# Attention backward as one stream of slots, and a guard moved from the MLP-down stage into the MLP forward

## The chip, the cores and the metric

The kernel runs on one core of one Trainium2 chip. The metric is the device time of one execution in microseconds (us). Medians are of several executions; one execution of each kernel comes with a profile and a trace. On one core the engines are TensorE (PE in the profile, with PEld for its weight loads, which overlap), VectorE (DVE), ScalarE (ACT), GpSimd (POOL) and SyncE (SP, which here only issues DMAs). Tiles lie in SBUF, the core's memory for them; matmuls write into PSUM buffers, which ACT and DVE read.

## The reference, cut to what matters

The program is a forward pass and its gradients: a layer norm, an attention block with 32 heads, a gated MLP whose output gates the attention's output, and the gradients of everything.

```python
x  = A_x                                   # [1, 2048, 576]
xn = layernorm(x)
# attention, H = 32 heads, Dh = 128, 2048 queries and keys; k_cache and v_cache are inputs
q  = (xn @ wq) -> heads
p  = softmax(q @ k_cache^T * Dh**-0.5)
s  = (p @ v_cache -> rows) @ wo
# MLP, F = 4608
h  = sigmoid(xn @ w_gate) * (xn @ w_up)
g  = silu(h @ w_down)
out = x + s * g
# returned: out and the gradients for x, k_cache, v_cache, wq, wo, w_gate, w_up, w_down
```

Of the kernel before, what the change touches and what calls it, by code (L numbers as in the profile page):

```python
# [95 lines left out]
def kernel(  # L96
# [72 lines left out]
    with tc.tile_pool(name="pa", bufs=1) as pa:  # L169
        wd_sb = pa.tile([P, FT, D], bf, name="wd_sb")  # L170
        with tc.tile_pool(name="a1w", bufs=1) as wp:
# [22 lines left out]
            with tc.tile_pool(name="a0", bufs=3) as sb0, tc.tile_pool(name="a0ps", bufs=2, space=PSUM) as ps0, \  # L194
# [23 lines left out]
                for grp in range(NFC // GRP):  # L218
                    for st in range(NT):
# [9 lines left out]
                        for c in range(GRP):  # L229
# [13 lines left out]
                            nc.scalar.activation(oma[:], g_ps[:], AF.Sigmoid, scale=-1.0)  # L243
                            nc.vector.tensor_tensor(h_row[:, cs], u_ps[:], a_row[:, cs], op=ALU.mult)
# [5 lines left out]
            a0x.release()  # L250

# [3 lines left out]
        with tc.tile_pool(name="gd", bufs=2) as gp:  # L255
            ksq = gp.tile([P, H], f32, name="ksq", bufs=1)
            wsq = gp.tile([P, DT], f32, name="wsq", bufs=1)
            nc.vector.memset(wsq[:], 0.0)

            def guard_k(h):  # L260
                kt_ = gp.tile([P, NT * P], bf, name="gk")
                nc.gpsimd.dma_start(kt_[:], A_k_cache[0, h].rearrange("(p t) d -> p (t d)", t=NT))
                nc.scalar.activation(kt_[:], kt_[:], AF.Square, accum_out=ksq[:, h:h + 1])

            def guard_w(i):
                d0, kd = dts[i]
                wt_ = gp.tile([P, HD], bf, name="gw")
                nc.gpsimd.dma_start(wt_[:kd, :], A_wq[d0:d0 + kd, :])
                nc.scalar.activation(wt_[:kd, :], wt_[:kd, :], AF.Square, accum_out=wsq[:kd, i:i + 1])

            def guard_end():
                gm = gp.tile([P, 2], f32, name="gm", bufs=1)
                nc.vector.tensor_reduce(gm[:, 0:1], ksq[:], axis=AX.X, op=ALU.max)
                nc.vector.tensor_reduce(gm[:, 1:2], wsq[:], axis=AX.X, op=ALU.add)
                nc.sync.dma_start(gd_d[0:1, :].rearrange("o p -> p o"), gm[:, 0:1])
                nc.sync.dma_start(gd_d[1:2, :].rearrange("o p -> p o"), gm[:, 1:2])
                gr = gp.tile([1, 2, P], f32, name="gr", bufs=1)
                nc.sync.dma_start(gr[:], gd_d[:, :].rearrange("(o a) p -> o a p", o=1))
                gs = gp.tile([1, 4], f32, name="gs", bufs=1)
                nc.vector.tensor_reduce(gs[:, 0:1], gr[:, 0, :], axis=AX.X, op=ALU.max)  # L280
                nc.vector.tensor_reduce(gs[:, 1:2], gr[:, 1, :], axis=AX.X, op=ALU.add)
                nc.vector.tensor_tensor(gs[:, 2:3], gs[:, 0:1], gs[:, 1:2], op=ALU.mult)
                nc.vector.tensor_scalar(gs[:, 3:4], gs[:, 2:3], (SAFE / SCALE) ** 2 / D, None, op0=ALU.is_le)
                nc.vector.tensor_copy(flag_i[:], gs[:, 3:4])

            with tc.tile_pool(name="a2h", bufs=4) as hp, \
                    tc.tile_pool(name="a2s", bufs=2) as sb, tc.tile_pool(name="a2ps", bufs=2, space=PSUM) as ps, \
                    tc.tile_pool(name="a2pt", bufs=2, space=PSUM) as pst:
                SG = ldiv(NT, 2)
                pend2 = []  # L290
                for sg in range(NT // SG):
                    grows = slice(sg * SG * P, (sg + 1) * SG * P)
                    got = sb.tile([P, SG, D], bf, name="got")
                    nc.gpsimd.dma_start(got[:], go2[grows, :].rearrange("(t p) d -> p t d", p=P))
                    g2 = sb.tile([P, SG, D], f32, name="g2")
                    dsil = sb.tile([P, SG, D], bf, name="dsil")
                    g2b = sb.tile([P, SG, D], bf, name="g2b")
                    ds_t = sb.tile([P, SG, D], bf, name="ds_t")
                    for sl in range(SG):
                        st = sg * SG + sl  # L300
                        srows = slice(st * P, (st + 1) * P)
                        hT_st = hp.tile([P, FT, P], bf, name="hT_st")
                        nc.sync.dma_start_transpose(hT_st[:], h_d[srows, :])
                        while len(pend2) > 1:
                            (t_, sl_, st_) = pend2.pop(0)
                            transpose_to(nc, pst, t_[:, sl_, :], D, dsT, st_ * P, ident, alt)
                        for j in range(st * H // NT, (st + 1) * H // NT):
                            guard_k(j)
                        if st < DT:
                            guard_w(st)  # L310
                        accs = [ps.tile([P, 512], f32, name=f"acc{j}") for j in range(len(ncs))]
                        for ft in range(FT):
                            for j, (n0, nn) in enumerate(ncs):
                                nc.tensor.matmul(accs[j][:, :nn], lhsT=hT_st[:, ft, :], rhs=wd_sb[:, ft, n0:n0 + nn],
                                                 start=(ft == 0), stop=(ft == FT - 1))
                        sig = sb.tile([P, D], f32, name="sig")
                        for j, (n0, nn) in enumerate(ncs):
                            nc.scalar.activation(sig[:, n0:n0 + nn], accs[j][:, :nn], AF.Sigmoid)
                            nc.vector.tensor_tensor(g2[:, sl, n0:n0 + nn], accs[j][:, :nn], sig[:, n0:n0 + nn], op=ALU.mult)
                        t1 = sb.tile([P, D], f32, name="t1")  # L320
                        nc.vector.scalar_tensor_tensor(t1[:], sig[:], 1.0, g2[:, sl, :], op0=ALU.subtract, op1=ALU.mult)
                        nc.vector.tensor_tensor(dsil[:, sl, :], sig[:], t1[:], op=ALU.subtract)
                        nc.vector.tensor_tensor(ds_t[:, sl, :], got[:, sl, :], g2[:, sl, :], op=ALU.mult)
                        pend2.append((ds_t, sl, st))
                    nc.gpsimd.tensor_copy(g2b[:], g2[:])
                    nc.gpsimd.dma_start(g2_d[grows, :].rearrange("(t p) d -> p t d", p=P), g2b[:])
                    nc.gpsimd.dma_start(dsil_d[grows, :].rearrange("(t p) d -> p t d", p=P), dsil[:])
                    nc.gpsimd.dma_start(ds_d[grows, :].rearrange("(t p) d -> p t d", p=P), ds_t[:])

                for (t_, sl_, st_) in pend2:  # L330
                    transpose_to(nc, pst, t_[:, sl_, :], D, dsT, st_ * P, ident, alt)
                guard_end()
# [6 lines left out]
    def attention(fast):  # L339
        with ExitStack() as es:  # L340
# [11 lines left out]
            skew = SKEW if fast else 2  # L352
# [82 lines left out]
            def prep_dot(hs, sc):  # L435
                if sc == 0:
                    hs.dOT = ld1.tile([P, S], bf, name="dOT")
                    hs.dOn = ld1.tile([P, NT, P], bf, name="dOn")
                gen_T(hs.woT, dsT, hs.dOT, sc, "v")
                nb = CH // P  # L440
                pe_transpose_blocks(lambda j: hs.dOT[:, j * P:(j + 1) * P], sc * nb, (sc + 1) * nb,
                                    lambda g, n: hs.dOn[:, g:g + n, :], "v")
# [10 lines left out]
            def scores(hs, qt, hf):  # L453
                qs = slice(qt * P, (qt + 1) * P)
                with tc.high_priority():
                    sp = ps_big.tile([P, HW_], f32, name="sp", tag="big")
                    for c in range(HW_ // CH):
                        nc.tensor.matmul(sp[:, c * CH:(c + 1) * CH], lhsT=hs.QT[:, qs],  # L458
                                         rhs=hs.KT[:, hf * HW_ + c * CH: hf * HW_ + (c + 1) * CH], start=True, stop=True)
                return sp  # L460

            def main1(hs, qt):
                Pq = slabp.tile([P, S], bf, name="Pq")
                hs.slabs[qt] = Pq
                rsp = stat.tile([P, NHF], f32, name="rsp")
                if fast:
                    for hf in range(NHF):
                        sp = scores(hs, qt, hf)
                        nc.scalar.activation(Pq[:, hf * HW_:(hf + 1) * HW_], sp[:], AF.Exp, scale=SCALE,  # L469
                                             accum_out=rsp[:, hf:hf + 1])  # L470
                else:
                    nm = stat.tile([P, NHF], f32, name="nm")
                    snegs = []
                    for hf in range(NHF):
# [424 lines left out]
```

## The kernel before: what the change touches

The stages run one after the other: MLP forward, MLP-down (with its gradient `ds`), attention for 32 heads (forward and backward, 61% of the time), then four stages of output projection and weight gradients, which the change leaves alone. All code and diffs in this document are condensed; `...` marks a cut, and lines that only name or index things are left out without a mark.

A *guard* decides at run time whether softmax may skip its row maximum: it needs a bound on the largest squared norm of a key and the sum of squares of `wq`. It reads 21 MB, squares it on ACT and sums it. Before, all of that sat inside the MLP-down stage, whose own input `hT_st` is a DMA transpose of `h`:

```python
def guard_k(h):                                   # one head's keys, 512 KB
    kt_ = gp.tile([P, NT * P], bf, name="gk")     # gp has 2 buffers
    nc.gpsimd.dma_start(kt_[:], A_k_cache[0, h].rearrange("(p t) d -> p (t d)", t=NT))
    nc.scalar.activation(kt_[:], kt_[:], AF.Square, accum_out=ksq[:, h:h + 1])
...
    hT_st = hp.tile([P, FT, P], bf, name="hT_st")           # MLP-down, 16 row tiles
    nc.sync.dma_start_transpose(hT_st[:], h_d[srows, :])
    ...
    for j in range(st * H // NT, (st + 1) * H // NT):
        guard_k(j)                                          # two heads per row tile
    if st < DT:
        guard_w(st)
    for ft in range(FT): ...                                # 72 matmuls
```

Attention works head by head in two phases of 16 query tiles (`qt`) of 128 rows. Phase 1 makes the scores `sp` in two halves of 1024 keys, takes the exponential on ACT into a slab `Pq` (128x2048), and transposes the slab by DMA (`PT`) for the product with V. Phase 2 makes `dp` in two halves, multiplies it into the slab on ACT and DVE, and transposes the slab again (`dST`) for the product with K. Between these come many narrow matmuls of 128 columns: tails (`acc<-Vn,PT` and `acc<-Kn,dST`), and the sums for the gradients of V and K (`acc<-dOn,Pq`, `acc<-Qn,Pq`).

```python
skew = 5                         # a slab's tail comes 5 tiles after its scores
def scores(hs, qt, hf):
    with tc.high_priority():     # the scheduler may put these ahead of other matmuls
        sp = ps_big.tile([P, HW_], f32, name="sp", tag="big")      # 2 PSUM buffers, shared with dp
        for c in range(HW_ // CH):
            nc.tensor.matmul(sp[:, c*CH:(c+1)*CH], lhsT=hs.QT[:, qs], rhs=hs.KT[...], ...)
def main2(hs, qt):
    for hf in range(NHF):
        with tc.high_priority(): dp = ...                           # 2 matmuls, as above
        if hf == NHF - 1:
            nc.vector.scalar_tensor_tensor(Pq[:, hsl], dp[:], hs.delta[...], Pq[:, hsl], op0=ALU.subtract, op1=ALU.mult)
        else:
            nc.scalar.activation(t[:], dp[:], AF.Identity, bias=hs.negdelta[...], scale=1.0)
            nc.vector.tensor_tensor(Pq[:, hsl], t[:], Pq[:, hsl], op=ALU.mult)
    hs.dST[qt] = transpose_slab(hs, qt, "dST")                      # DMA transpose on SP
def post1(hs):                                                      # start of phase 2
    nc.gpsimd.tensor_scalar(hs.rsc[:], hs.rinv_all[:], SCALE, None, op0=ALU.mult)
    nc.gpsimd.tensor_tensor(hs.Qn[:], hs.Qn[:], hs.rsc[:].unsqueeze(2).to_broadcast([P, NT, P]), op=ALU.mult)
...
for h in range(H):                 # the loop
    for i in range(NT + skew):     # phase 1: main1(i), tail1(i - skew), parts of dK of the head before, dV
        ...
    for i in range(NT + skew):     # phase 2: main2(i), tail2(i - skew), rest of dV, dK, next head's preparation
        ...
```

## Time and profile before

The median is 5703.88 us (5701.29 to 5713.11, 3 runs; 5705.36 with a fourth). The profiled run spans 5680.1 us. The stages, from the starts of their last matmuls in the trace (worked out from the trace's records, as are all per-head figures below):

| stage | us before | ends at |
|---|---|---|
| MLP forward | 346.2 | 346.2 |
| MLP-down, with the guard | 251.5 | 597.7 |
| attention | 3487.9 | 4085.6 |
| the rest | 1594.5 | 5680.1 |

The table of stretches of the kernel before gives busy time per engine in each stretch, then the granted clock of TensorE, the busy share of the DMA engines and GB/s:

```profile
45.00:347.00 302.00, 300.02 (x1398) 137.64 (x1425) 163.27 (x321) 184.26 (x327) 74.64 (x138) 1.00 0.52 201
347.00:605.00 258.00, 167.15 (x1208) 84.45 (x1232) 62.20 (x106) 94.34 (x122) 60.66 (x85) 0.82 0.94 198
605.00:4090.00 3485.00, 3314.47 (x39843) 2521.31 (x40352) 1849.14 (x4223) 2049.67 (x3585) 1013.70 (x1759) 1.00 1.06 188
```

The columns are PE, PEld, DVE, ACT, POOL. The MLP forward is PE-bound (300 of 302 us). The MLP-down stage is not: PE works 167 of 258 us while the DMA engines are 94% busy. Its waits say on what (engine, line, what it waited for: us in total, times, longest):

```profile
ACT gk L263 <- DMA gk<-in_A_k_cache_dram: 74.3, 16, 11.8
PE acc L314 <- DMA hT_st<-h_d: 44.0, 5, 22.2
```

In attention PE looks 95% busy, yet records of matmuls overlap (a 128-column one lasts 219 ns on average where the next starts 56 ns later), so that hides what is lost. The timeline shows starts; `acct` are transposes of 128x128 blocks made on PE. The kernel before on PE, first in phase 1, then in phase 2 (start us, us, engine, line, operation, out<-in, how many in a row, idle before and its releaser):

```profile
2702.41 0.59 PE L458 MATMUL sp<-KT,QT 128*128 128x512 bf16 x2
2702.84 0.66 PE L369 MATMUL acct<-ident,QT 128*128 128x128 bf16 x9
2703.42 0.59 PE L458 MATMUL sp<-KT,QT 128*128 128x512 bf16 x2
2703.85 0.33 PE L369 MATMUL acct<-ident,QT 128*128 128x128 bf16 x3
2704.01 0.44 PE L562 MATMUL acc<-dOn,Pq 128*128 128x128 bf16 x5
2704.42 0.59 PE L458 MATMUL sp<-KT,QT 128*128 128x512 bf16 x2
...
2727.08 1.22 PE L500 MATMUL acc<-Vn,PT 128*128 128x128 bf16 x19
2728.49 1.02 PE L523 MATMUL dp<-VT,dOT 128*128 128x512 bf16 x4 [0.19 <-ACT t L529]
2729.35 1.22 PE L500 MATMUL acc<-Vn,PT 128*128 128x128 bf16 x19
2730.77 0.38 PE L523 MATMUL dp<-VT,dOT 128*128 128x512 bf16 x1 [0.19 <-ACT t L529]
```

A score half comes every 1.00 us: the scores run ahead in a burst as fast as ACT's exponentials (one per 1.00 us) free the two PSUM buffers. In phase 2 four `dp` matmuls come at once and then wait for ACT and DVE. The next lines are waits of the kernel before between 630 and 4060 us. The first shows the end of each burst: ACT has no free slab and waits up to 12.8 us, once a head, until the matmuls on old slabs have freed one.

```profile
ACT Pq L469 <- PE acc L562: 395.3, 31, 12.8
PEld L523 <- issue: 152.2, 514, 0.7
PE dp L523 <- ACT t L529: 57.9, 294, 0.5
PE acct L369 <- DVE dOT L42: 31.2, 64, 0.8
```

Matmuls that follow each other without a wait start every 55.8 ns with 128 columns and every 215.2 to 215.8 ns with 512, which is N/2.4 + 2.45 ns (N columns). Summed over the 40,352 matmuls of the attention that is 3111 us; from first to last start the trace has 3475 us. So 364 us are stalls of PE: by the trace about 190 us before `dp`, 135 us before `sp`, the rest mostly before the `dOT` transposes.

### The profile page before, as it was taken

To read this page: it belongs to the slowest core of one execution; us is meant where nothing else is said; L and a number is where in the kernel's file an instruction comes from. 1 tells how busy PE (TensorE), PEld (TensorE's weight loads), DVE (VectorE), ACT (ScalarE), POOL (GpSimd) and SP (SyncE) were. 2 spreads that over 40 slices of the span, in tenths; PEclk is the share of its full clock that TensorE was granted. 3 is DMA by queue.
4 is the path that set the end of the run, shared out by engine and by line. 5 is a ranking of instruction groups with operands and counts; after the bars stand their busy time and mean duration, and the time that the engine had idled before them with its cause. 6 is when DMAs were issued, how large, how long until landed. Compare 5 with 4: busy or idle time off the path is not lost.

```text
span 5680.1 us, 129804 instructions
## 1 busy us (share of the span) xinstructions
PE 5290.7 (93%) x54473; PEld 3695.7 (65%) x55220; DVE 2472.9 (44%) x5723; ACT 2601.1 (46%) x4668; POOL 1429.2 (25%) x2398
## 2 busy tenths in 40 slices
PE   8977899999999999999999999999789999999999
PEld 3433577777777777777777777777656777744454
DVE  5532445545545555554554554555433333211011
ACT  7543565565565555555556556556422222200000
POOL 2222223223223323322322322322212222211000
PEclk9988999999999999999999999999999999999999
DMA  7489899999999999999999999999955555583875
GB/s 275 182 214 207 159 188 186 191 191 184 190 187 188 190 188 188 188 190 187 185 194 187 187 191 190 184 189 186 213 174 169 174 174 174 178 240 123 179 148 111
DMA packets 2715209, 1053.93 MB, mean 186 GB/s; under 512 B 2521185, under 2 KB 2641634, under 8 KB 2711986
## 3 DMA queue, kind: packets, MB, share of 16 engines
q1 hardware_dynamic: 2626050, 743.33, 72.4%
q0 software_dynamic: 88560, 302.14, 16.9%
q8 instruction: 434, 7.11, 0.5%
q14 instruction: 165, 1.35, 0.1%
HBM read 213.91 MB, written 201.00 MB: 73 GB/s over the span
## 4 chain that ended last, share of the span: by engine, by line
PE 60%; ACT 18%; issue 12%; DVE 3%; DMA 3%; POOL 2%; SPq 1%; ACTq 0%; POOLq 0%; DVEq 0%
PE acc L562 11%; ACT Pq L469 9%; PE acc L840 7%; ACT t L529 7%; PE dp L523 5%; PE accw L768 5%; PE acc L500 5%; PE acc L537 5%; PE sp L458 4%; PE acc L427 3%; PE dh L745 3%; PE accq L808 2%; PE acc L799 2%; PE accd L757 2%; PE acc L707 2%
## 5 line engine op out<-in xcount | busy, mean ns | idle before, releaser
L469 ACT ACTIVATE Pq<-sp 128x1024 bf16<-128x1024 f32 x1024 | 1044.6, 1065 | 434.9 <-PE acc L562 395.3
L562 PEld LDWEIGHTS <-Pq 128*128 128x128 bf16 x16384 | 1002.3, 98 | 153.3
L529 ACT ACTIVATE t<-dp,negdelta 128x1024 bf16<-128x1024 f32 x512 | 573.7, 1120 | 431.6 <-PE dp L523 161.0
L526 DVE SCALAR_TENSOR_TENSOR Pq<-dp,delta,Pq 128x1024 bf16<-128x1024 f32 x512 | 653.4, 1281 | 151.0 <-PE acc L562 119.7
L523 PE MATMUL dp<-VT,dOT 128*128 128x512 bf16 x1823 | 531.7, 377 | 81.1 <-ACT t L529 58.3
L562 PE MATMUL acc<-dOn,Pq 128*128 128x128 bf16 x8192 | 587.5, 219 | 3.4
L458 PE MATMUL sp<-KT,QT 128*128 128x512 bf16 x1859 | 565.4, 377 | 21.3 <-ACT Pq L469 1.5
L562 PE MATMUL acc<-Qn,Pq 128*128 128x128 bf16 x8192 | 580.3, 219 | 3.4
L537 PE MATMUL acc<-Kn,dST 128*128 128x128 bf16 x8192 | 571.5, 219 | 8.1 <-DMA dST<-Pq 2.5
L500 PE MATMUL acc<-Vn,PT 128*128 128x128 bf16 x8192 | 572.4, 219 | 6.9
L537 PEld LDWEIGHTS <-dST 128*128 128x128 bf16 x8192 | 504.2, 98 | 108.1 <-DMA dST<-Pq 3.3
L500 PEld LDWEIGHTS <-PT 128*128 128x128 bf16 x8192 | 500.8, 98 | 88.7
L530 DVE TENSOR_TENSOR Pq<-t,Pq 128x1024 bf16<-128x1024 bf16 x512 | 422.3, 830 | 82.5 <-ACT t L529 55.6
L484 DVE TENSOR_REDUCE rs_all<-rsp 128x1 f32<-128x2 f32 x512 | 78.1, 152 | 762.5 <-ACT Pq L469 759.2
L489 POOL TENSOR_SCALAR dOn<-dOn,rinv_all 128x128 bf16<-128x128 bf16 x512 | 306.3, 608 | 316.6 <-DVE rinv_all L485 130.4
L523 PEld LDWEIGHTS <-dOT 128*128 128x128 bf16 x2048 | 192.5, 97 | 234.7 <-issue 152.9
L504 DVE TENSOR_SCALAR o_n<-acc,rinv_all 128x128 bf16<-128x128 f32 x512 | 177.6, 347 | 304.7 <-PE acc L500 304.0
L768 PEld LDWEIGHTS <-xn_all 128*128 128x128 bf16 (+1 forms) x2880 | 281.5, 100 | 40.3 <-issue 11.2
L458 PEld LDWEIGHTS <-QT 128*128 128x128 bf16 x2048 | 197.9, 97 | 154.1 <-issue 64.3
L541 ACT ACTIVATE dq_n<-acc,rsc 128x128 bf16<-128x128 f32 x512 | 192.4, 376 | 224.0 <-PE acc L537 224.0
L568 ACT COPY part<-acc 128x512 f32<-128x512 f32 x256 | 151.3, 591 | 239.9 <-PE acc L562 239.9
L494 POOL DMA_DIRECT2D dq_d<-dq_n x128 | 97.6, 763 | 630.2 <-ACT dq_n L541 616.1
(181 smaller groups left out, 7144.5 us busy)
## 6 DMA issues: line engine op xcount, KB each, us to landing
out_dram<-kvo POOLq DMA_DIRECT2D x256, 128.0 KB, 4.0
h_d<-h_row POOLq DMA_DIRECT2D x48, 384.0 KB, 2.7
a_d<-a_row POOLq DMA_DIRECT2D x48, 384.0 KB, 2.6
b_d<-b_row POOLq DMA_DIRECT2D x48, 384.0 KB, 3.2
a_blk<-a_d SPq DMA_DIRECT2D x18, 1024.0 KB, 5.8
b_blk<-b_d SPq DMA_DIRECT2D x18, 1024.0 KB, 18.8
h_blk<-h_d POOLq DMA_DIRECT2D x18, 1024.0 KB, 11.3
du_d<-du_blk POOLq DMA_DIRECT2D x18, 1024.0 KB, 9.5
```

The lines of the kernel that those rows point to most:

```text
L458: nc.tensor.matmul(sp[:, c * CH:(c + 1) * CH], lhsT=hs.QT[:, qs], rhs=hs.KT[:, hf * HW_ + c * CH: hf * HW_ + (c + 1) * CH], start=True, st ...
L469: nc.scalar.activation(Pq[:, hf * HW_:(hf + 1) * HW_], sp[:], AF.Exp, scale=SCALE, accum_out=rsp[:, hf:hf + 1])
L489: nc.gpsimd.tensor_scalar(hs.dOn[:, qt, :], hs.dOn[:, qt, :], hs.rinv_all[:, qt:qt + 1], None, op0=ALU.mult)
L500: nc.tensor.matmul(op_[:, 0, :], lhsT=PT[:, kt, :], rhs=hs.Vn[:, kt, :], start=(kt == 0), stop=(kt == NT - 1))
L523: nc.tensor.matmul(dp[:, c * CH:(c + 1) * CH], lhsT=hs.dOT[:, qs], rhs=hs.VT[:, hf * HW_ + c * CH: hf * HW_ + (c + 1) * CH], start=True, s ...
L526: nc.vector.scalar_tensor_tensor(Pq[:, hsl], dp[:], hs.delta[:, qt:qt + 1], Pq[:, hsl], op0=ALU.subtract, op1=ALU.mult)
L529: nc.scalar.activation(t[:], dp[:], AF.Identity, bias=hs.negdelta[:, qt:qt + 1], scale=1.0)
L530: nc.vector.tensor_tensor(Pq[:, hsl], t[:], Pq[:, hsl], op=ALU.mult)
L537: nc.tensor.matmul(qp[:, 0, :], lhsT=dST[:, kt, :], rhs=hs.Kn[:, kt, :], start=(kt == 0), stop=(kt == NT - 1))
L562: nc.tensor.matmul(self.tile[:, j, :], lhsT=self.slabs[qt][:, kt * P:(kt + 1) * P], rhs=self.rhs[:, qt, :], start=(qt == self.lo), stop=(q ...
L768: nc.tensor.matmul(acc[:kd, :], lhsT=xn_all[:, st, d0:d0 + kd], rhs=blk_[:, st, :], start=(st == 0), stop=(st == NT - 1))
L840: nc.tensor.matmul(accs[sl][j][:, :nn], lhsT=ch[:, kk, sl * P:(sl + 1) * P], rhs=wT[:, k0 + kk, n0:n0 + nn], start=(kidx == 0), stop=(kidx ...
```

## The change

The intent is to take those stalls out. All heads and both phases become one list of slots (2 x 16 per head). Every slot holds one score pair (two `sp` halves or two `dp` halves), and all other matmuls are put into slots with their column counts; a half is followed by half of the slot's other columns. No `high_priority` is left, so the order of the program is the order on PE. A tail is cut in two parts, and some copies change engine. The tails of phase 1 now run on into phase 2's slots, and those of phase 2 into the next head's.

The guard moves into the MLP forward: 84 pieces of up to 256 KB, loaded from SP, one piece per 512 columns, squared on ACT between the sigmoids of that stage. The MLP-down stage then has the DMA engines for itself.

```diff
+        gp = tc.alloc_tile_pool(name="gd", bufs=2)
+        def guard_k(h, hf):                               # half a head
+            v = gp.tile([P, GQ], bf, name="gk")
+            nc.sync.dma_start(v[:].rearrange("p (t d) -> p t d", d=P), src)
+            nc.scalar.activation(v[:], v[:], AF.Square, accum_out=ksq[:, 2 * h + hf:2 * h + hf + 1])
 ...
                             nc.scalar.activation(a_row[:, cs], g_ps[:], AF.Sigmoid)
                             nc.scalar.activation(oma[:], g_ps[:], AF.Sigmoid, scale=-1.0)
+                            if grp > 0 and guards:
+                                guards.pop(0)()
 ...                                                       (guard removed from the MLP-down stage)
-                with tc.high_priority():
-                    sp = ps_big.tile([P, HW_], f32, name="sp", tag="big")
+            def main1(hs, qt, hf):                        # one half
+            def main2(hs, qt, hf):                        # one half
+            def tail1(hs, qt, part): ...                  # 8 of 16 matmuls
+            def plan(h):                                  # put(slot, columns, function)
+                b1, b2 = 2 * NT * h, 2 * NT * h + NT
+                    put(b1 + qt + skew, NT * P // 2, lambda qt=qt: tail1(hd(), qt, 0))
+                    ...
-            for h in range(H):
-                for i in range(n_it): ...                 (the loop shown above)
+            while slot < 2 * NT * H or units:
+                us = units.pop(slot, []); total = sum(c for c, _ in us); run = 0
+                for hf in range(NHF):
+                    (main1 if r < NT else main2)(heads[h], r % NT, hf)
+                    while us and (hf == NHF - 1 or run < total * (hf + 1) // NHF):
+                        c, fn = us.pop(0); fn(); run += c
+                slot += 1
```

## The prediction

> **What bounds it now.** By the table of stretches, attention (about 605 to 4090 us) is 61% of the span: 107.5 us per head, PE busy 95%. Busy hides what is lost, because a matmul's record includes its drain. In the PE timeline sixteen 128-column matmuls start every 0.89 us (55.8 ns each) and 512-column ones every 0.216 us. That is N/2.4 + 2.5 ns, the isolated gap of the Trainium skill ("TensorE: Matmul & The Clock Gate", Back-to-back issue gap), not the sustained 81 ns that page also gives. Summed over the program's 40,352 attention matmuls this is 3111 us; first to last start is 3475 us. The 364 us between are stalls: about 190 us just before dp halves (typically 0.27 to 0.36 us), 135 us before sp halves, 45 us at the dOT to dOn transposes. The scores come in bursts, limited by ACT (one exp per 1.00 us) or by ACT and DVE (a dp pair per 2.27 us), then pause.
>
> **What the change does.** The instruction order of the new build has one half (2 matmuls) after each 8 to 24 narrow ones, so a half comes every 1.33 us or more and its PSUM buffer is reused after 2.7 us. Consumers need less: exp 1.00 us per half; DVE 1.8 us per dp pair plus about 0.55 us of kvo and junk per slot. No PE work is added or removed. So nearly all 320 us of score stalls and the 30 to 45 us at dOn should go.
>
> **What takes their place.** The SP timeline: 1024 slab transposes, 2.97 us each, next issue within 0.2 us of the last one's end in 73% of cases, idle about 10% in all. Back to back with no other DMA in between they come every 2.46 us; with a 128 KB store in between 3.6 us, so the queues share the engines, as the Trainium skill says ("DMA: Bandwidth & Descriptors", Issuing engines are not separate DMA queues). Fitted to the mean mix of stores this gives 3.13 to 3.19 us per slab, an estimate: 3200 to 3260 us for 1024, above PE's 3111. I expect transposes to become the limit at about 101 to 102 us per head: attention about 3275 us, a gain of 200 us, not 364. The chain of waits would then hold waits of acc (L500/L537's successors) for DMA PT and dST, 2.5 us today.
>
> **Guard.** The MLP-down stage (346 to 604 us) takes 258 us for about 150 us of PE (16 tiles of 72 matmuls, 8.9 us each, plus transposes); the rest is hT_st waiting for DMA, which guard loads (21 MB) share: landing 18.6 us median. Without them I expect 165 to 170 us: gain 90 us. In the MLP forward ACT idles 1.07 us per 512 columns and a half-size square with its accumulator read costs about 1.0 us (half of 1.9 to 2.1), so it just fits; two load buffers at 2.16 us each may wait. Cost: 5 us (0 to 35).
>
> **Sum.** 5704 − 200 − 90 + 5 ≈ 5419 us, range 5310 to 5525. Chances: faster over 2% 0.94, within 0.05, slower 0.01.
>
> **Right if:** sp and dp idle entries (L529, L469 as releasers of PE) nearly vanish; per-head period 100 to 103 us; SP back to back over 90%; DMA PT/dST among PE's releasers with 100 us or more; the stage with hT_st shrinks to about 165 us; later stages unchanged.
>
> **Wrong if:** transposes spaced evenly suffer less from stores than in bursts, so PE reaches 98 us per head (total near 5310); or late slabs stall PE in program order and the stalls add (near 5520); or DVE, with 2.35 of 2.7 us per slot early in phase two, holds dp; or the guard's squares in ACT's strict order wait for their loads and hold the sigmoids.

## The result, and the profile after

The changed kernel takes 5494.39 us (5486.65 to 5499.84, 4 runs). The ratio to before is 0.9628, with a 95% interval of 0.9611 to 0.9644. A ratio here is the mean time of one kernel's fast runs over that of the other's of the same rounds, so not quite the ratio of the medians.

| stage | us before | us after | difference |
|---|---|---|---|
| MLP forward | 346.2 | 417.8 | +71.6 |
| MLP-down | 251.5 | 167.8 | −83.7 |
| attention | 3487.9 | 3317.1 | −170.8 |
| the rest | 1594.5 | 1595.3 | +0.8 |
| sum (profiled runs) | 5680.1 | 5498.0 | −182.1 |

The medians differ by 211 us, not 182, because the profile of before fell at the fast end of its runs. A caution for all that follows: single profiled runs with the very same attention code differ by up to 17 us in that stage (3300.5, 3307.7 and 3317.1 us in three kernels below), so a difference of that size in one profile means nothing.

The table of stretches of the kernel after, cut at its own stage ends (columns as before):

```profile
45.00:418.00 373.00, 312.03 (x1397) 139.32 (x1424) 163.93 (x328) 265.83 (x494) 74.16 (x137) 0.96 0.62 222
418.00:600.00 182.00, 152.00 (x1228) 80.74 (x1252) 60.79 (x98) 16.54 (x50) 45.50 (x56) 0.92 0.75 173
600.00:3905.00 3305.00, 3121.62 (x39697) 2481.82 (x40334) 1874.21 (x4192) 2139.28 (x3617) 1019.68 (x1752) 1.00 1.14 197
```

The MLP-down stage did what was expected. The MLP forward got 81 us more of ACT work (265.8 for 184.3) and is no longer PE-bound: PE is busy 312 of 373 us (12 us more than before, at a granted clock of 0.96 for 1.00). Why is in its waits (45 to 440 us) and in the timeline of one piece:

```profile
ACT gk L183 <- DMA gk<-in_A_k_cache_dram: 50.2, 24, 3.7
ACT gk L190 <- DMA gk<-in_A_wq_dram: 20.2, 7, 8.0
PE g_ps L276 <- ACT oma L282: 50.2, 26, 7.5
```

```profile
202.81 1.24 PE L279 MATMUL u_ps<-wu_sb,xnT 128*128 128x512 bf16 x5
204.14 1.06 ACT L183 ACTIVATE gk<-gk 128x1024 bf16<-128x1024 bf16 x1 [2.55 <-DMA gk<-in_A_k_cache_dram]
205.10 0.19 ACT L183 ACTIVATION_READ_ACCUMULATOR gk<-gk 128x1 f32 x1
205.19 0.58 ACT L280 ACTIVATE a_row<-g_ps 128x512 bf16<-128x512 f32 x1
206.31 1.28 PE L276 MATMUL g_ps<-wg_sb,xnT 128*128 128x512 bf16 x5 [2.26 <-ACT oma L282]
```

ACT stands 2.55 us before a square whose data has not landed. The sigmoid behind it waits as well, though its matmul was done, so no PSUM buffer comes free, and PE stands 2.26 us. The work itself fits, though barely: PE needs 2.16 us per 512 columns (10 matmuls of 0.216 us), and ACT starts two sigmoids and a square again every 2.00 us where nothing waits (180.66 and 182.66 us in the same trace). It is the order that doesn't. With two buffers a load starts only when the square two pieces back is done; that leaves it about 2 x 2.16 − 1.06 = 3.3 us (an estimate from these lines), and the median landing is 4.1 us, the longest 14.0.

In attention, the same two views as before. The timeline of PE, first phase 1, then early in phase 2:

```profile
2690.64 0.59 PE L466 MATMUL sp<-KT,QT 128*128 128x512 bf16 x2
2691.07 1.06 PE L570 MATMUL acc<-dOn,Pq 128*128 128x128 bf16 x16
2691.97 0.59 PE L466 MATMUL sp<-KT,QT 128*128 128x512 bf16 x2
2692.40 1.06 PE L510 MATMUL acc<-Vn,PT 128*128 128x128 bf16 x16
...
2705.67 0.59 PE L535 MATMUL dp<-VT,dOT 128*128 128x512 bf16 x2
2706.44 1.07 PE L510 MATMUL acc<-Vn,PT 128*128 128x128 bf16 x16 [0.17 <-DMA PT<-Pq]
2708.70 0.38 PE L535 MATMUL dp<-VT,dOT 128*128 128x512 bf16 x1 [1.20 <-DVE Pq L538]
```

The waits between 630 and 3880 us:

```profile
PEld L510 <- DMA dST<-Pq: 80.3, 61, 10.1
PE acc L510 <- DMA dST<-Pq: 60.9, 52, 9.6
PE dp L535 <- DVE Pq L538: 53.6, 59, 1.5
PEld L510 <- DMA PT<-Pq: 47.4, 55, 4.0
PE acc L510 <- DMA PT<-Pq: 25.4, 29, 3.5
```

A score half now comes every 1.33 us, with sixteen narrow matmuls after it. The stalls before scores are gone: 1012 of 1020 recorded `sp` halves and 955 of 1024 `dp` halves start within 10 ns of the ideal. PE's stalls fell from 364 to 193 us, and the waits that remain are new ones: tails waiting for their DMA transpose, which stood at 2.5 us for `dST` on the page before. SP's timeline of the kernel before:

```profile
2689.62 34.40 SPq L450 DMA_TRANSPOSE PT<-Pq  x10
```

And of the kernel after:

```profile
2699.29 9.67 SPq L460 DMA_TRANSPOSE PT<-Pq  x3
2709.06 2.70 SPq L460 DMA_TRANSPOSE dST<-Pq  x1
```

A row holds several issues with the gaps between them. By the single records, an issue occupies SP for 3.08 us on average (2.97 before). After, 95.3% of the issues start within 0.2 us of the last one's end (72.7% before), one per 3.206 us, which is 102.6 us for a head's 32. PE's 3111 us are 97.2 us per head. SP is not just waiting for slabs: no issue starts before its slab is ready, and a slab lies ready 3.6 us (`PT`) or 5.1 us (`dST`) on average before SP takes it up.

The other new wait, PE at `dp` for DVE, sits early in phase 2. There the profile shows an odd pair (the timeline of POOL and DVE of the kernel after):

```profile
2702.20 0.69 DVE L543 TENSOR_TENSOR Pq<-t,Pq 128x1024 bf16<-128x1024 bf16 x1 [0.69 <-ACT t L542]
2703.09 3.61 POOL L529 TENSOR_TENSOR Qn<-Qn,rsc 128x2048 bf16<-128x2048 bf16 x1
2704.40 2.84 DVE L543 TENSOR_TENSOR Pq<-t,Pq 128x1024 bf16<-128x1024 bf16 x1
```

The DVE multiply that takes 0.69 us takes 2.84 us next to the scaling of `Qn` on POOL, and ends 0.54 us after that does. So it is in 31 of the 32 heads, and in all 32 of the kernel before: each of these long multiplies ends 0.54 to 0.55 us after the scaling. The Trainium skill ("SBUF — State Buffer", Who interferes with whom and Summary: rules for kernel authors) says that a VectorE instruction with two SBUF inputs contends with a GpSimd instruction that reads SBUF, and that the one that comes second is blocked until the first is done. This trace agrees.

### The profile page after: what moved, and what is told of

It reads as the page before. It is cut to its first block, busy times and chain, and to the rows that moved or that the text cites. A ratio compares the mean times of both kernels' runs of the same rounds, so it can differ in the third digit from the quotient of the medians.

```text
span 5498.0 us, 129982 instructions
## 1 busy us (share of the span) xinstructions
PE 5095.5 (93%) x54343; PEld 3654.3 (66%) x55220; DVE 2497.0 (45%) x5692; ACT 2695.0 (49%) x4794; POOL 1420.1 (26%) x2361
## 5 line engine op out<-in xcount | busy, mean ns | idle before, releaser
L484 ACT ACTIVATE Pq<-sp 128x1024 bf16<-128x1024 f32 x1024 | 1048.1, 1024 | 328.2 <-PE sp L466 205.5
L542 ACT ACTIVATE t<-dp,negdelta 128x1024 bf16<-128x1024 f32 x512 | 571.5, 1116 | 278.9 <-POOL negdelta L524 160.7
L510 PE MATMUL acc<-Kn,dST 128*128 128x128 bf16 x8192 | 554.0, 220 | 69.3 <-DMA dST<-Pq 65.6
L535 PE MATMUL dp<-VT,dOT 128*128 128x512 bf16 x1728 | 541.5, 380 | 53.7 <-DVE Pq L538 53.6
L510 PEld LDWEIGHTS <-dST 128*128 128x128 bf16 x8192 | 490.4, 98 | 140.3 <-DMA dST<-Pq 85.7
L510 PE MATMUL acc<-Vn,PT 128*128 128x128 bf16 x8192 | 547.8, 219 | 33.0 <-DMA PT<-Pq 25.6
L570 PE MATMUL acc<-dOn,Pq 128*128 128x128 bf16 x8192 | 546.5, 219 | 10.3 <-DVE o_n L50 0.2
L466 PE MATMUL sp<-KT,QT 128*128 128x512 bf16 x1762 | 547.7, 379 | 1.2 <-ACT Pq L484 1.2
L570 PE MATMUL acc<-Qn,Pq 128*128 128x128 bf16 x8192 | 541.3, 219 | 3.4
L50 DVE TENSOR_SCALAR o_n<-acc,rinv_all 128x128 bf16<-128x128 f32 x352 | 123.5, 351 | 299.3 <-PE acc L510 299.3
L580 POOL DMA_DIRECT2D out_dram<-kvo x256 | 148.9, 582 | 406.3 <-DVE kvo L579 404.0
L276 PE MATMUL g_ps<-wg_sb,xnT 128*128 128x512 bf16 x694 | 185.8, 392 | 59.8 <-ACT oma L282 50.2
L535 PEld LDWEIGHTS <-dOT 128*128 128x128 bf16 x2048 | 164.3, 98 | 83.0 <-issue 61.0
```

The costliest lines, as they stand in the source:

```text
L466: nc.tensor.matmul(sp[:, c * CH:(c + 1) * CH], lhsT=hs.QT[:, qt * P:(qt + 1) * P], rhs=hs.KT[:, hf * HW_ + c * CH: hf * HW_ + (c + 1) * CH ...
L484: nc.scalar.activation(Pq[:, hsl], sp[:], AF.Exp, scale=SCALE, accum_out=hs.rsp[:, hf:hf + 1])
L510: nc.tensor.matmul(hs.acc[:, 0, :], lhsT=T[:, kt, :], rhs=rhs[:, kt, :], start=(kt == 0), stop=(kt == NT - 1))
L535: nc.tensor.matmul(dp[:, c * CH:(c + 1) * CH], lhsT=hs.dOT[:, qt * P:(qt + 1) * P], rhs=hs.VT[:, hf * HW_ + c * CH: hf * HW_ + (c + 1) * C ...
L570: nc.tensor.matmul(self.tile[:, j, :], lhsT=self.slabs[qt][:, kt * P:(kt + 1) * P], rhs=self.rhs[:, qt, :], start=(qt == self.lo), stop=(q ...
```

## The experiments

The first theory, called A: in attention the transposes on SP's queue, slowed (as it supposes) by the stores beside them, set the pace, with PE and its remaining waits just below; the moved guard costs what it costs because ACT waits for loads. Rivals, called B and C in the expectations where they were named: that something on the compute engines holds the attention (the `dp` waits, the Qn scaling, or the spacing of the halves), and that it is the latency of single transposes rather than their rate. Every kernel gave correct outputs. Diffs are against the changed kernel.

### The two halves of the change apart

`att_only` is the new attention with the old guard; `guard_only` is the old attention with the moved guard.

> The new attention with the old guard (in the MLP-down stage). The stage bounds of the two traces give attention 173 us of the gain and the guard move about 12 us (72 us lost in the MLP forward, 84 us won in the MLP-down stage). If the parts are independent: about 5530 us, ratio 0.968 to 0.972. If the new attention only pays together with the moved guard: above 5600 us.

> The old attention with the moved guard. Independent parts: about 5693 us, ratio 0.996 to 1.001, the MLP forward ending near 418 us instead of 346 us and the MLP-down stage 180 us instead of 264 us. If the prediction's term (90 us won, 5 us lost) was right and the loss came from elsewhere: about 5620 us.

`att_only` took 5523.33 us, ratio 0.970 (0.9657 to 0.9743). `guard_only` took 5670.36 us, ratio 0.9934 (0.9909 to 0.996), about 23 us better than the 5693 expected. The product, 0.9636, is the whole change's 0.9628 within the intervals, so the halves add. By the traces, `guard_only` has the changed kernel's first two stages (414.0 and 168.2 us) and the old attention (3490.0); `att_only` the reverse (348.2, 255.9, 3307.7). The guard's move is worth about 38 us by the ratio and 12 us by the two profiles. In the same rounds the runs with the old guard spread over 27 us (before) and those of `guard_only` over 5; that the old MLP-down stage varies in length and was short in the profile of before would fit, but no run shows it. The clocks point the same way: longer runs of the kernel before have the lower mean clock (5680.53 us with 0.983, 5728.96 with 0.978), and between 45 and 4090 us its profile shows less than 1.00 in the MLP-down stage alone (0.82).

### gk3: a third guard buffer

```diff
-        gp = tc.alloc_tile_pool(name="gd", bufs=2)
+        gp = tc.alloc_tile_pool(name="gd", bufs=3)
```

> After with three buffers for the guard's loads instead of two. Theory: in the MLP forward ACT waits, in its strict order, for a load that could only be issued when its buffer was free (70 us of ACT idle on DMA gk; load 3.9 us to landing); with three in flight a piece has 6.5 us, ACT's idle on DMA gk falls below 25 us and the total to 5425 to 5465 us. Rival: ACT is full (about 2.2 us of work per 2.16 us), or the DMA engines are; then the idle moves elsewhere and the total stays above 5480 us.

It took 5454.31 us, ratio 0.9558 (0.9524 to 0.9593). ACT's waits for the loads fell from 70.4 us to 31.0 us, not quite below the 25 expected (the waits of this kernel, 45 to 440 us):

```profile
ACT gk L183 <- DMA gk<-in_A_k_cache_dram: 23.0, 18, 2.6
ACT gk L190 <- DMA gk<-in_A_wq_dram: 8.0, 6, 2.1
```

The MLP forward fell from 417.8 to 396.7 us. So the wait for loads is a cause of the loss, and more buffers a cure for part of it. It isn't one for one: 39 us less waiting gave 21 us. The rest of the gain in this profile is 17 us of attention with the same code, which is within the spread named above. About 50 us of the loss remain, of which 31 are ACT's waits; the rest was not traced in full, but PE's own busy time (314 us, at a clock of 0.98) is part of it.

### pet2: two slabs per head transposed on PE instead of by DMA

If transposes set the pace, taking away two of 32 should gain.

```diff
+    PET = (9, 13)
-                hs.PT[qt] = transpose_slab(hs, qt, "PT")
+                if qt not in PET:
+                    hs.PT[qt] = transpose_slab(hs, qt, "PT")
+            def pe_slab(hs, qt):       # 16 transposes on PE, two copies on DVE
+                hs.PT[qt] = wpt.tile([P, NT, P], bf, name="PTe", tag="PT")
+                pe_transpose_blocks(lambda j: hs.slabs[qt][:, j * P:(j + 1) * P], 0, NT, lambda g, n: hs.PT[qt][:, g:g + n, :], "v")
+                for qt in PET:
+                    put(b1 + qt + 1, NT * P, lambda qt=qt: pe_slab(hd(), qt))
```

> After with 2 of a head's 32 slab transposes made by PE matmuls (and DVE copies) instead of DMA. Theory A, throughput of the DMA transposes (3.2 us per slab, back to back 95%) sets the pace: 30 slabs are 96 us per head, PE's own need becomes 99 us, so 2 to 3 us per head are won: 5395 to 5440 us. Theory B, PE's own work or its waits for ACT and DVE set the pace: 1.8 us per head more PE work, 5535 to 5560 us.

It took 5533.02 us (5528 to 5542), slower than the change, so the expectation of theory A failed; the time lies just under the range of theory B. The queue was relieved: it was back to back in only 66% of cases and idle 441 us (37 us in the changed kernel). But PE did not get faster. Its waits (630 to 3900 us) moved:

```profile
PE dp L542 <- DVE Pq L545: 88.8, 80, 3.7
PE acc L517 <- DMA dST<-Pq: 24.6, 10, 5.1
```

The waits for transposes fell from 86 to 25 us, those for DVE rose from 54 to 89, and PE had 57 us more work (64 slabs of 0.89 us). In one place looked at closely DVE stood 5.04 us in its order before a `kvo` addition (`kvo` holds finished parts of the gradients of K and V) whose buffer's earlier store had not landed, and PE then stood 3.02 us before `dp`. So transposes are not the only limit: PE lies just under them, in the changed kernel at about 100.6 us per head (an estimate: 3304.5 us from first to last start, less its 86 us of waits for transposes, over 32).

### kvo1: one store of 512 KB in place of four of 128 KB

The stores of the gradients of K and V share the DMA engines with the transposes, and write runs of 1 KB; one store writes runs of 4 KB.

```diff
-                            fo_ = stg.tile([P, 4, P], bf, name="kvo")
-                            nc.vector.tensor_tensor(fo_[:, :j + 1, :], self.tile[...], self.part[...], op=ALU.add)
-                            nc.gpsimd.dma_start(self.out_dram...[:, k0:kt + 1, :], fo_[:, :j + 1, :])
+                            if k0 == 0:
+                                self.fo = stg.tile([P, NT, P], bf, name="kvo", bufs=1)
+                            nc.vector.tensor_tensor(self.fo[:, k0:kt + 1, :], ...)
+                            if self.kt == NT:
+                                nc.gpsimd.dma_start(self.out_dram.rearrange("(p t) d -> p t d", t=NT), self.fo[:])
```

> After with each dV or dK half-result stored by one 512 KB DMA (4 KB runs) instead of four of 128 KB (1 KB runs). No compute changes. Theory A with stores sharing the engines (an interval with a store of about 128 KB lasts 3.5 us, without any 2.7 us): 3 to 5 us per head less DMA time, of which PE's own pace (97 us plus 2 us of dp waits) lets 2 to 4 us through: 5375 to 5440 us. Rival (the transposes are slowed by something of their own, bytes are the same): 5480 to 5510 us.

It took 5474.73 us, ratio 0.9606 (0.9572 to 0.9641), which overlaps the change's. The pace of the slabs was 3.194 us (3.206), attention 3303.9 us. The expected gain did not come (the time lies 5 us under the rival's range): the length of the stores' runs is not the cause of the slabs' 3.2 us. That leaves the bytes stored beside them, or something of the transposes' own. The traces speak for the bytes: in the changed kernel a gap-free interval takes 2.68 us on average where no store lies in it and 3.48 us with 70 to 140 KB, and in `kvo1` 2.72 and 3.43. No run varied the bytes, so this is not shown by experiment.

### negv and together: two suspects on the compute engines

`negv` puts the negation of `delta`, for which ACT waited 160.7 us in the changed kernel, on DVE instead of POOL. `together` puts both halves of a pair at the start of the slot, as a burst of four matmuls.

```diff
-                nc.gpsimd.tensor_scalar(hs.negdelta[...], hs.delta[...], -1.0, None, op0=ALU.mult)
+                nc.vector.tensor_scalar(hs.negdelta[...], hs.delta[...], -1.0, None, op0=ALU.mult)
```
```diff
-                    while us and (hf == NHF - 1 or run < total * (hf + 1) // NHF):
+                    while us and hf == NHF - 1:
```

> After with negdelta computed on DVE instead of POOL. In the trace the early dp halves of the second phase stall PE twice a head by about 1 us (61 us in all) because ACT's t waits for negdelta, which on POOL sits behind the 3.6 us scaling of Qn. Theory A: these stalls lie inside time that the DMA transposes need anyway; PE waits for DMA instead: 5475 to 5500 us. Rival (PE waits add up): 5425 to 5445 us. Both: waits of dp for DVE fall from 54 us to under 15 us.

> After, but both score halves at the start of a slot instead of one at its start and one in its middle. Theory A (DMA sets a slot of 3.2 us): a pair needs its two buffers back once per slot, ACT 2.0 us or DVE 1.8 us after them, so few waits return and those lie inside DMA time: 5490 to 5530 us; what won is one pair per slot, not the even spacing. Rival (spacing is what won): stalls before sp and dp return by over 150 us and the total rises to 5600 us or more.

They took 5493.6 us (ratio 0.9642, 0.9615 to 0.9669) and 5487.06 us (0.9635, 0.9602 to 0.9668): no change from 0.9628. In `negv` the `dp` waits stayed at 52.5 us, so the negation was not their cause. `together` says something about the change itself: the even spacing of the two halves within a slot is not what won the time. That leaves one pair per slot, in one stream, in place of bursts that run ahead, as what won it; but this is by elimination, since no run separates it from the other parts of the change (tails cut in two and running on into the next phase, copies on other engines).

### skew6: transposes get one slot more

If single late transposes held PE, more time between a slab and its tail should help.

```diff
-    SKEW = 5
+    SKEW = 6
-            wpt = pool("wpt", 7 if fast else 4)
+            wpt = pool("wpt", 8 if fast else 4)
```

> After with tails 6 slots behind the scores instead of 5, and 8 transposed-slab buffers instead of 7 (7 and 9 did not fit the memory). Theory A (the DMA transposes' throughput sets the pace): total within 0.5% of after, 5470 to 5515 us, back to back over 90%, 3.19 us per slab. Theory C (enough throughput, now and then a late transpose): a slot of 3.2 us more slack removes most of the 110 us of waits for DMA PT and dST: 5390 to 5430 us.

It took 5547.73 us (5521 to 5561), 1% slower and outside the ranges of both theories, and attention in its profile 3338.2 us. The slabs came every 3.228 us, back to back in 97.7% of cases; PE's waits for `dST` were longer and fewer (86.0 us in 33, at most 10.4), and those for both kinds grew from 86 to 96 us. So the gain that theory C named did not come: more time between slab and tail does not help a queue that runs without gaps. Why the kernel was slower, and not the same, is open, and as long as it is, this run speaks against latency without settling it. A skew of 7 did not fit in SBUF (14 KB were needed and 12.3 left) and did not run.

### extra: a 33rd transpose per head

```diff
+                if qt == 10:
+                    transpose_slab(hs, qt, "extra")      # nobody reads it
```

> After with one more DMA transpose per head (slab 10 a second time, into a buffer that nobody reads): 33 instead of 32, no compute changed. Theory A: 3.2 us more per head, 102 us in all: 5580 to 5610 us. Theory B (PE with its waits for ACT and DVE sets the pace, transposes have slack): under 5520 us.

It took 5567.01 us (5558 to 5570), 73 us more than the change and 13 us under the range of theory A: 2.3 us per head for one more transpose of 3.2 us. Attention grew by 70.2 us to 3387.3, which is 2.2 us per head. PE's waits (630 to 3800 us) show where:

```profile
PE acc L512 <- DMA PT<-Pq: 85.9, 80, 3.2
PE acc L512 <- DMA dST<-Pq: 85.0, 62, 5.7
PE dp L537 <- DVE Pq L540: 7.5, 11, 1.2
```

PE had no more work, so time on the queue does become time of the kernel, which rival B excluded. Why 2.2 us and not 3.2 is in the queue's own pace: 33 slabs came every 3.177 us (96.5% without a gap), so a head took the queue 104.8 us, 2.2 more than the 102.6 of the changed kernel. A slab more brings no store with it, and 3.2 us is the mean of intervals with and without stores; the expectation had priced it at the mean. The longer pace also covers most waits for DVE (down to 7.5 us from 51.4 in the same window of the changed kernel). The extra slab also holds one of the seven buffers for transposed slabs while it is made; this run does not separate that.

### qnv: the scaling of Qn on DVE, in 16 pieces

This removes the POOL instruction that blocks DVE.

```diff
-                nc.gpsimd.tensor_tensor(hs.Qn[:], hs.Qn[:], hs.rsc[:]..., op=ALU.mult)
+            def scale_qn(hs, qt):
+                nc.vector.tensor_scalar(hs.Qn[:, qt, :], hs.Qn[:, qt, :], hs.rinv_all[:, qt:qt + 1], SCALE, op0=ALU.mult, op1=ALU.mult)
+                for qt in range(NT):
+                    put(b1 + max(qt + 2, q(NTH + 2) + 1 + qt // 4), 0, lambda qt=qt: scale_qn(hd(), qt))
```

> After with the scaling of Qn taken from POOL (one 128x2048 operation, 3.61 us) and done by DVE in 16 pieces of 128x128 as the row sums come. In the trace of after a DVE multiply that takes 0.68 us lasted 2.84 us while that POOL operation ran and ended just after it, and in the same slots PE waits 2.0 us per head before dp. Moving negdelta alone left those 2 us in place. Expected: the waits of dp for DVE fall from 54 us to under 15 us, the multiply's maximum to under 1.5 us; by theory A the total hardly moves (5470 to 5500 us), by theory B it falls by 60 us (5425 to 5445 us).

It took 5483.44 us, ratio 0.9607 (0.9579 to 0.9635). The waits (PE, 630 to 3800 us) turned into others:

```profile
PE acc L510 <- DMA dST<-Pq: 81.8, 62, 3.2
PE acc L510 <- DMA PT<-Pq: 29.4, 34, 2.2
PE dp L537 <- DVE Pq L540: 6.9, 23, 0.4
```

The `dp` waits are gone (51.4 us in the same window of the changed kernel, now 6.9), so the scaling on POOL was their cause. The waits for the transposes grew by 25 us, and the time hardly moved. This is what two limits close together look like: take the lower one away and the time goes to the upper one.

### pet1q: both limits together

Now take the `Qn` scaling off POOL (as in `qnv`) and one transpose per head off the queue (as in `pet2`, with `PET = (10,)`).

> qnv plus one of a head's 32 slab transposes made on PE. DMA then needs 31 x 3.19 = 98.9 us per head, PE 97.2 + 0.9 = 98.1 us with its dp waits gone. Theory A (a bound of DMA at 102.2 us just above one of PE at 101 us; both must be moved): 5385 to 5430 us. If pet2's loss came from the PE transposes themselves (their DVE copies, PSUM buffers): 5480 us or more.

It took 5427.33 us (5424 to 5429), ratio 0.9507 (0.9475 to 0.9538), 67 us better than the change. Attention is 3242.1 us, 65.7 us less than in `qnv`: 2.05 us per head for one transpose less, nearly the price of one more in `extra`. The queue's time per head fell by as much: 31 slabs at 3.233 us are 100.2 us, against 102.3 in `qnv`. Waits for `dST` are at 30.9 us. That `pet2` lost and this one gained cannot be put down to the scaling alone, for the number and the places of the slabs differ as well.

### best1: all that helped

This is `pet1q` with the third guard buffer and the single store.

> The changed kernel with everything that helped: one slab per head transposed on TensorE and the Qn scaling on VectorE (as in pet1q, 5427 us), three guard buffers (gk3 alone was worth about 40 us in the first stage) and one 512 KB store per half result (kvo1 alone was worth 10 to 20 us). The guard's stage and the attention are apart in time, so the gains should add: 5365 to 5400 us. A time above 5410 would say that the guard's gain is given back later or that the gains overlap. All outputs correct.

It took 5402.0 us (5369.84 to 5408.98), ratio 0.9448 (0.9402 to 0.9494): the fastest here, 2 us above the range expected. Against `pet1q` the MLP forward fell from 421.2 to 387.9 us and attention stayed (3244.7 for 3242.1). So in these profiles the third buffer did all of it and the single store nothing, which agrees with the unchanged pace in `kvo1`.

## Why the prediction was right or wrong

The direction and the range were right: 5494.39 us, in 5310 to 5525. The middle, 5419, was 75 us too low. By the profiles the sum was 103 us too low, and two thirds of that lie in one term; that the medians forgive 29 us of it is luck. Going through the sum, by the profiles:

| term | predicted | profiles |
|---|---|---|
| attention | −200 | −171 |
| MLP-down without the guard | −90 | −84 |
| MLP forward with the guard | +5 (0 to 35) | +72 |
| the rest | 0 | +1 |

- **"Cost: 5 us (0 to 35)" is the step that failed.** The prediction read correctly that the squares just fit into ACT's idle time, and it named the risk ("two load buffers at 2.16 us each may wait", and again under "Wrong if"), but priced it at 5. The runs show 70.4 us of ACT waiting for the loads and 71.6 us lost, and 21 to 33 us won back by one more buffer. So what was priced wrongly is the wait, and not ACT's work. The arithmetic could have been done: a time of about 3.3 us for a load against landings that the old trace gave as 8.8 us for pieces twice the size under heavier load.
- **Attention: mechanism right, size 29 us off** (17 us of which is no more than the spread between profiles). "I expect transposes to become the limit at about 101 to 102 us per head": they take 102.6 us, back to back in 95.3% of cases (over 90% was named), and `extra`, `qnv` and `pet1q` show that they set the pace. Their pace, 3.206 us, was just above the fitted 3.13 to 3.19. The prediction did not foresee that PE with its waits would be as close under it, so that neither limit can be lifted alone.
- **"sp and dp idle entries nearly vanish"** is half right. On the page the idle before `sp` fell from 21.3 to 1.2 us, that before `dp` only from 81.1 to 53.7, with a new releaser. The prediction had listed that DVE might hold `dp` early in phase two. It did, but because POOL's scaling blocked it, which stood in the old trace too (32 long multiplies) and nobody read, and `qnv` shows that it was not what limited the time.
- **"DMA PT/dST among PE's releasers with 100 us or more"**: 86.3 us on PE, with 127.7 us on its weight loads, which overlap. Right in kind, but under the 100 on PE. The chain of waits was of no use after the change: its shares cover only about 43% of the span.
- **The stage with `hT_st`** came to 167.8 us (165 to 170 was named), and the later stages did not move. Both right.
- The gain by the medians, 211 us, is 29 above that of the profiles. That much lies in which run the profile of before was, and not in a stage.

## What to carry to other kernels

When one engine's stalls are taken away, ask which queue would then run without gaps and what its rate is with the traffic that shares it: here 364 us of stalls gave 171 us, because the DMA transposes stood at 102.6 us per head behind PE's 97.2. In attention, of the runs here only the one that took work off the queue and unblocked PE together gained further. One more transpose cost 2.2 us and not the mean 3.2, so price a step by what it adds to the queue and not by the queue's mean pace. Work moved into an engine's idle time, in front of other work in its order, must have its data there beforehand; the idle time is not the price, the late load is, and one more buffer won back 21 to 33 us of 72 here. Test two limits that lie close together by easing both at once, and test a suspected limit also by adding to it: if it is the limit, the time must grow by what the queue's own time grows, as it did here (2.2 us per head in both).

## What the Trainium skill lacked or had wrong

- "TensorE: Matmul & The Clock Gate", Back-to-back issue gap: it gives about 81 ns (128 columns) and 131 ns (512 columns) per matmul as what a real stream of weight loads and matmuls sustains, and calls N/2.4 + 2.5 ns the isolated gap. This stream, with a weight load for each narrow matmul, starts 16 of them in 0.89 us (55.8 ns each) and two wide ones in 0.43 us, wherever in attention it does not stall.
- "DMA: Bandwidth & Descriptors", Latency and other measured facts: for DMA transposes it gives 261 GB/s, and about 350 to 400 where contiguous. Here transposes of 512 KB from SBUF to SBUF come every 2.46 us where no store lies between (kernel before), which is 213 GB/s, and every 3.206 us on average in the changed kernel, 164 GB/s.
- The same page says that the queues share the same engines (Issuing engines are not separate DMA queues), but not what that costs a transpose: with 70 to 140 KB of stores between two of them the interval was 3.58 us instead of 2.46 in the kernel before (3.48 instead of 2.68 after). No page has that.
- "SBUF — State Buffer", Who interferes with whom, had it right: a 0.69 us DVE multiply took 2.84 us next to a 3.61 us GpSimd multiply.
